# Dividing attention's outputs instead of its score blocks, pairing outputs, and loading the mask sizes on GpSimd's queue, in a fused attention and two-layer FFN kernel

## The chip, the cores and the metric

The kernel runs on one core of one Trainium2 chip. A core has five engines that each run their own stream of instructions: TensorE (PE, matrix products), VectorE (DVE), ScalarE (ACT), GpSimd (POOL) and SyncE (SP, which here only issues DMAs). The metric is the device time of one execution in microseconds (us); lower is better.

## The reference

Local and global attention with a distance bias, followed by two feed-forward layers:

```python
scores = scale * np.matmul(q, k.transpose(0, 1, 3, 2))     # q, k, v: 2 x 8 heads x 768 x 64
keep = is_global | is_local        # k < n_global (8), or 0 <= q - k < n_local (96)
scores = np.where(keep, scores + bias, -1e9)               # bias = -slope[head] * distance
a = np.exp(scores - np.max(scores, axis=-1, keepdims=True))
a = a / (np.sum(a, axis=-1, keepdims=True) + 1e-09)
x = np.matmul(a, v)                                        # as 1536 tokens x 512
h = x @ w_in;  x = (h * sigmoid(h)) @ w_out                # 512 -> 2048 -> 512
h = x @ w_in2; return np.maximum(0.01 * h, h) @ w_out2     # again 512 -> 2048 -> 512
```

`n_global` and `n_local` are inputs that the kernel reads at run time, as 64-bit integers; the weights come as 64-bit floats. A branch at the end of the program computes the attention in another way for sizes that the fast path does not cover; it does not run here.

## The kernel before

**Attention.** The work is cut into 24 units: a batch, a third of its queries (256) and a pair of heads; unit n counts pairs of heads fastest, then thirds, then batches. A unit passes through these steps, each a function of the code:

- `ld_qk`, `ld_v` (L893, L920): SyncE's queue (and for the first unit's k ScalarE's) loads q, k and v for two units at a time.
- `st_T` (L936 to L951): TensorE turns q and k by four transposes (products with the identity) into the PSUM tile `pt`; ScalarE copies q into `qT` with its scale, ScalarE or VectorE copies k into `kT` (helper L222 or L224), and VectorE spreads k's first columns, the global ones, to the other blocks (L948) where the unit is in the first third.
- `st_S` (L979): the scores, eight products into two PSUM tiles `s`. Each reads only 64 of the partitions, one head's. In the same task the outputs of the unit two back (`LAG`) are formed right behind them, see `st_AV`.
- `st_P`: VectorE scans each of four score blocks (L1012: adds the mask and keeps the minimum of its negative, the maximum, in `nm`) into `A`; ScalarE takes the exp and its sum (L1019, `su`); VectorE forms the reciprocal `rs` (L1025, L1026), 128 queries by 4 blocks, and multiplies each block of A by its column (L1035).
- `st_A` (L1052): TensorE transposes A into `pa`; ScalarE or VectorE copies it to `AT` (four buffers).
- `st_AV` (L1078): 6 or 8 products of v and `AT` into `pv`, 64 x 256 for each head, one head in the upper and one in the lower half of the partitions. ScalarE copies that to the high part of the layers' input `x` (L1090), VectorE the rest, `pv` minus the high part, to the low part (L1093).

**Layers.** Products are formed in three passes over high and low parts, in tiles `ph` (L600, first product of a layer), `po` (L655, second) and `pq` (L490, a form with fewer products). The weights are loaded by SyncE's queue into `st`, and brought to a high and a low part by ScalarE and VectorE (L273 to L288).

**Opening.** GpSimd builds the identity and the mask's constants; SyncE's queue loads q of the first unit, then n (`load_n`, L79, two DMAs into `nraw`), then more. VectorE makes floats of n in five small steps (`masks_n`, L828 to L832), then the mask (L839, L840, L843, L844). TensorE, with nothing to do yet, runs dummy products of zeros into `wps` (`warm_up`, L878): eight before the first transposes, two and one behind the first and the second unit's, and 16 more that the planner puts where TensorE would wait.

**Order.** A planner in Python (`Sched`) holds each task with its engine, an assumed duration, a priority (lower first; mostly the unit's number plus an offset), what it depends on and which buffers it needs. It plays the program through with these durations and writes each engine's order; that order is fixed when the program is built. A priority or an assumed duration thus changes only the order.

Of the kernel before, what the change touches and what calls it, by code (L numbers as in the profile page):

```python
# [26 lines left out]
def kernel(  # L27
# [40 lines left out]
    ident = const.tile([P, P], F32, name="ident")  # L68
    make_identity(nc, ident)

    warm = const.tile([P, 1], F32, name="warm")
    nc.vector.memset(warm, 0.0)
# [25 lines left out]
    def flags():  # L98
        nc.vector.tensor_scalar(fl[:, 0:1], nlf, 1.0, None, op0=ALU.is_lt)
        nc.vector.tensor_scalar(fl[:, 1:2], nlf, float(NPV + 1), None, op0=ALU.is_gt)  # L100
        nc.vector.tensor_scalar(fl[:, 2:3], ngf, float(NG), None, op0=ALU.is_gt)
        nc.vector.tensor_reduce(fl1, fl, axis=mybir.AxisListType.X, op=ALU.max)
        nc.vector.tensor_copy(flag, fl1)

    PASSES = ((0, 0), (1, 0), (0, 1))
    LAG = 2
    ADEPS = 0.1

# [11 lines left out]
    class Sched:  # L120
# [7 lines left out]
        def add(self, eng, dur, fn, prio, deps=(), bufs=(), at=0.0, land=ADEPS, dma=False):  # L128
            t = {"eng": (eng,) if isinstance(eng, str) else eng, "dur": dur if isinstance(dur, tuple) else (dur,),
                 "fn": fn, "prio": prio, "deps": [d for d in deps if d is not None], "bufs": bufs, "at": at,  # L130
                 "land": land, "dma": dma or eng == "SP", "out": [], "i": len(self.tasks), "state": 0}
# [8 lines left out]
        def run(self):  # L140
# [3 lines left out]
            for t in self.tasks:  # L144
                for e in t["eng"]:
                    free.setdefault(e, 0.0)
                    ready.setdefault(e, [])
# [4 lines left out]
            seq, dma = 0, 0.0  # L152
# [11 lines left out]
            now = 0.0  # L164
            while len(order) < len(self.tasks):
                for e in free:
# [20 lines left out]
                    end = free[e] = now + t["dur"][t["eng"].index(e)]  # L187
# [40 lines left out]
    class Moe:  # L228
# [233 lines left out]
        def unit_quad(self, ns, L, pair):  # L462
# [19 lines left out]
            def prod(c, A, Bx, first, deps=()):  # L482
# [15 lines left out]
                for kk in range(2):  # L498
                    m = add("PE", 3 * (0.2267 if two else 0.1185), fn(kk), self.pos, (wd, m, *Bx[kk][1], *deps), (wt_, bank[c], Bx[kk][0]))
# [83 lines left out]
        def unit_in(self, n, j, c0=0, w=TG):  # L583
# [42 lines left out]
            for kk in range(NKK):  # L626
                xd = [q for (a0, a1, q) in self.xdone[L][gi][kk] if a0 < c0 + w and c0 < a1]
                last = add("PE", 3 * 0.2267 * r, mm(kk), self.pos, (wt, last, *xd), (wb, ph, xs[kk]))
# [7 lines left out]
        def unit_out(self, n, e, c0=0, w=TG):  # L636
# [22 lines left out]
            for j in range(FPP):  # L659
                wb, wt = self.w["out", L, part * FPP + j]  # L660
                g, gt = self.g[n, j]
                m = add("PE", 3 * 0.2267 * r, mm(j), self.pos, (m, wt, *gt), (po, wb, g))
# [112 lines left out]
    SIZES = {"st": 2, "f": 4, "wi": 4, "wo": 4, "g": 4, "t": 2, "ps": 8, "qT": 3, "A": 2, "AT": 4, "tl": 4, "gl": 2,  # L775
# [9 lines left out]
    with ExitStack() as es:  # L785
# [10 lines left out]
        apool = lambda name, bufs=1: ea.enter_context(tc.tile_pool(name=name, bufs=bufs))  # L796
# [3 lines left out]
        sm = apool("sm", 4)  # L800
# [312 lines left out]
        for n in range(NU - LAG, NU):  # L1113
            st_AV(n)[2](None)
# [151 lines left out]
```

## Time and profile before

| | us |
|---|---|
| three runs | 607.74, 605.6, 605.74 |
| median of the runs | 605.74 |
| span of the profiled execution | 606.2 |
| TensorE busy in it | 596.1 (98%) |
| VectorE busy | 528.4 (87%) |
| ScalarE busy | 305.4 (50%) |
| GpSimd busy | 3.7 (1%) |

The profile is one execution, recorded by the hardware. A line number with an L is a line of the kernel before. A timeline row gives when an instruction or a row of equal ones starts and how long it takes; in square brackets stands the engine's idle time before it and who released it. An engine that appears as SPq or ACTq is its queue issuing DMAs. "PEld" is the loading of TensorE's stationary operand, which overlaps its products. The chain of waits is followed back from the last instruction, at each step to what released it.

### The profile page before, as it was taken

To read this page: it belongs to the slowest core of one execution; us is meant where nothing else is said; L and a number is where in the kernel's file an instruction comes from. 1 tells how busy PE (TensorE), PEld (TensorE's weight loads), DVE (VectorE), ACT (ScalarE), POOL (GpSimd) and SP (SyncE) were. 2 spreads that over 40 slices of the span, in tenths; PEclk is the share of its full clock that TensorE was granted. 3 is DMA by queue.
4 is the path that set the end of the run, shared out by engine and by line. 5 is a ranking of instruction groups with operands and counts; after the bars stand their busy time and mean duration, and the time that the engine had idled before them with its cause. 6 is when DMAs were issued, how large, how long until landed. Compare 5 with 4: busy or idle time off the path is not lost.

```text
span 606.2 us, 9115 instructions
## 1 busy us (share of the span) xinstructions
PE 596.1 (98%) x3266; PEld 490.0 (81%) x3267; DVE 528.4 (87%) x1213; ACT 305.4 (50%) x682; POOL 3.7 (1%) x20
## 2 busy tenths in 40 slices
PE   8999999999999999999999999999999999999996
PEld 4678777778888888888888888898898889888985
DVE  4999999877999999995999999899999997978551
ACT  4789887876654435432555554556343433333110
POOL 2000000000000000000000000000000000000000
PEclk9999999999999999999999999999999999999999
DMA  8875568310012332322231111322132322010112
GB/s 180 185 174 141 136 167 203 71 36 1 0 36 70 105 105 69 106 69 70 69 105 35 36 35 36 105 69 85 54 105 71 104 70 69 6 65 1 70 55 90
DMA packets 72676, 49.43 MB, mean 82 GB/s; under 512 B 50480, under 2 KB 67120, under 8 KB 72624
## 3 DMA queue, kind: packets, MB, share of 16 engines
q1 hardware_dynamic: 71536, 48.51, 28.6%
q8 instruction: 28, 0.46, 0.3%
q10 hardware_dynamic: 1088, 0.26, 0.2%
q14 instruction: 24, 0.20, 0.1%
HBM read 45.62 MB, written 3.15 MB: 80 GB/s over the span
## 4 chain that ended last, share of the span: by engine, by line
PE 94%; DVE 3%; DMA 2%; ACT 1%; issue 0%; ACTq 0%
PE po L655 43%; PE pq L490 29%; PE ph L600 10%; PE s L979 3%; PE pa L1052 3%; PE pv L1078 3%; PE pt L936 2%; DMA st<-in_moe_w_in_dram 1%; DVE A L1012 1%; PE wps L878 1%; DMA q<-in_q_dram 1%; DVE A L1035 0%; DMA k<-in_k_dram 0%; ACT AT L222 0%; ACT A L1019 0%; DVE f L279 0%
## 5 line engine op out<-in xcount | busy, mean ns | idle before, releaser
L655 PE MATMUL po<-g,wo 128*128 128x512 f32 x576 | 141.5, 392 | 0.0
L655 PE MATMUL po<-wo,g 128*128 128x512 f32 (+1 forms) x588 | 136.2, 385 | 0.0
L655 PEld LDWEIGHTS po<-wo,g 128*128 128x128 f32 x588 | 107.7, 188 | 21.0
L655 PEld LDWEIGHTS po<-g,wo 128*128 128x128 f32 x576 | 106.9, 188 | 21.7 <-DVE wo L288 0.2
L600 PE MATMUL ph<-x,wi 128*128 128x512 f32 (+1 forms) x336 | 77.6, 366 | 0.9 <-DVE wi L288 0.6
L505 DVE TENSOR_TENSOR tl<-tl,pq 128x512 f32<-128x512 f32 (+1 forms) x110 | 64.3, 585 | 10.3 <-PE pq L490 5.3
L600 PEld LDWEIGHTS ph<-x,wi 128*128 128x128 f32 x336 | 56.4, 188 | 11.0 <-DVE wi L288 1.2
L490 PE MATMUL pq<-xs,ws 128*128 128x512 f32 x252 | 62.3, 389 | 0.0
L490 PEld LDWEIGHTS pq<-xs,ws 128*128 128x128 f32 x252 | 47.3, 188 | 9.8
L273 ACT ACTIVATE st<-st 128x512 f32<-128x512 f32 x64 | 42.9, 670 | 23.5 <-DMA st<-in_moe_w_out_dram 13.2
L1019 ACT ACTIVATE A<-A,nm 128x256 f32<-128x256 f32 (+1 forms) x96 | 46.1, 483 | 12.1 <-DVE nm L1012 11.9
L687 DVE SCALAR_TENSOR_TENSOR yp<-po,yp 128x512 f32<-128x512 f32 x60 | 40.7, 686 | 9.4 <-PE po L655 9.1
L279 DVE SCALAR_TENSOR_TENSOR f<-st,f 128x512 int32<-128x512 int32 x64 | 43.9, 687 | 0.9
L282 DVE SCALAR_TENSOR_TENSOR f<-st,f 128x512 int32<-128x512 int32 x64 | 43.8, 684 | 0.4
L575 ACT ACTIVATE g<-tl 128x512 fp32r<-128x512 f32 x40 | 25.0, 630 | 37.5 <-DVE tl L570 29.0
L490 PE MATMUL pq<-xn,wi 128*128 128x512 f32 (+1 forms) x192 | 43.1, 336 | 0.0
L1012 DVE CUSTOM_DVE_ANT_0 A<-s,mask 128x256 f32<-128x256 f32 (+1 forms) x96 | 34.7, 393 | 3.9 <-PE s L979 3.7
L222 ACT ACTIVATE wo<-f 128x512 fp32r<-128x512 f32 x30 | 18.9, 630 | 34.6 <-PE po L655 17.2
L490 PEld LDWEIGHTS pq<-xn,wi 128*128 128x128 f32 x192 | 32.3, 189 | 4.5
L578 DVE TENSOR_TENSOR g<-tl,g 128x512 fp32r<-128x512 f32 x40 | 27.1, 686 | 5.1 <-ACT g L575 4.8
L575 ACT ACTIVATE g<-t 128x512 fp32r<-128x512 f32 x32 | 20.1, 630 | 19.7 <-PE po L655 10.8
L276 DVE TENSOR_SCALAR f<-st 128x512 int32<-128x512 int32 x64 | 26.7, 420 | 1.6 <-ACT st L273 1.6
(119 smaller groups left out, 883.2 us busy)
## 6 DMA issues: line engine op xcount, KB each, us to landing
st<-in_moe_w_in_dram SPq DMA_DIRECT2D x32, 512.0 KB, 3.8
st<-in_moe_w_out_dram SPq DMA_DIRECT2D x32, 512.0 KB, 3.6
vd<-in_v_dram SPq DMA_DIRECT2D x24, 128.0 KB, 2.8
q<-in_q_dram SPq DMA_DIRECT2D x22, 128.0 KB, 3.1
k<-in_k_dram SPq DMA_DIRECT2D x22, 128.0 KB, 3.4
out_dram<-yo SPq DMA_DIRECT2D x11, 256.0 KB, 2.1
vp<-in_v_dram SPq DMA_DIRECT2D x20, 96.0 KB, 2.7
vp<-in_v_dram SPq DMA_DIRECT2D x20, 32.0 KB, 2.4
```

Of the source, the lines that this page charges most:

```text
L273: eng.activation(hf, hf, AF.Copy, scale=2.0 ** -112)
L279: eng.scalar_tensor_tensor(fi(), lo(), 29, fi(), op0=ALU.logical_shift_right, op1=ALU.bitwise_or)
L282: eng.scalar_tensor_tensor(fi(), hi(), -(2 ** 31), fi(), op0=ALU.bitwise_and, op1=ALU.bitwise_or)
L490: eng.matmul(bank[c]()[:, :w], wt_()[:, a, f0:f0 + P], x()[:, b, c0:c0 + w], start=(first and kk == 0 and i == 0), stop=(kk == 1 and i == ...
L505: eng.tensor_tensor(dst[0]()[:, dst[1]], a[0]()[:, a[1]], b[0]()[:, b[1]], op=op)
L575: eng.activation(g()[:, 0, :], t(), AF.Copy)
L578: eng.tensor_tensor(g()[:, 1, :], t(), g()[:, 0, :].bitcast(F32), op=ALU.subtract)
L600: eng.matmul(ph()[:, :w], wv[:, a, kk, :], xs[kk]()[:, b, cs], start=(kk == 0 and i == 0), stop=(kk == NKK - 1 and i == 2),)
L655: eng.matmul(po()[:, :w], lhsT, rhs, start=(j == 0 and i == 0), stop=(j == FPP - 1 and i == 2))
L687: eng.scalar_tensor_tensor(dst()[:, cs], po()[:, :w], scale, y()[:, cs], op0=ALU.mult, op1=ALU.add)
L1012: eng.tensor_tensor_reduce(A()[:, i, j, c0:256], s[j]()[:, i, c0:256], mask0 if c0 else mask, -QSCALE * SLOPE[2 * hp + j], 3.0e38, ALU.add ...
L1019: eng.activation(a, a, AF.Exp, bias=nm()[:, x:x + 1], scale=-1.0, accum_out=su()[:, x:x + 1])
```

## The change

1. **n** is loaded by GpSimd's queue, in the first two instructions of its program, and no longer by SyncE's.
2. **Early first scores.** The dummies around the second unit's transposes are two of 256 columns ahead and one of 512 behind, instead of three of 512 behind; the first unit's k is copied by VectorE; dummies are products with a broadcast 128-column tile of zeros, and so the fill of zeros is shorter.
3. **Division.** A is no longer multiplied by the reciprocal. It is transposed as the exp left it. A new step `st_R` transposes `rs` on TensorE (`pr`, 4 x 128), copies it on ScalarE (`rT`), sends it to DRAM (`rd`) by a DMA on GpSimd's queue and reads it back by two more, each spreading two rows over 64 partitions (`R`, 128 x 256, three buffers). VectorE multiplies the output in `pv` by `R`, ScalarE copies the product to the high part of `x`, VectorE forms the low part from it.
4. **Paired outputs.** From unit 12 on the outputs of two units are formed in one task, behind every second unit's scores; the last pair stands alone. `AT` has six buffers instead of four.
5. **Planner.** Scans get the priority n - 1.63 (n + 0.1 before), other offsets, assumed durations and due times of weights change, and the planner counts a price for going from one kind of product to another.

```diff
+    nraw = const.tile([P, 2, 2], I32, name="nraw")
+    def load_n(eng, x):
+        eng.dma_start(out=nraw[:, x], in_=(n_global, n_local)[x].bitcast(I32).partition_broadcast(P))
+    for x in range(2):
+        load_n(nc.gpsimd, x)
     ident = const.tile([P, P], F32, name="ident")
     make_identity(nc, ident)
-    def load_n(eng):
-        for x, src in enumerate((n_global, n_local)):
-            eng.dma_start(out=nraw[:, x], in_=src.bitcast(I32).partition_broadcast(P))
...
+    SOLO = 24
+    PAIRS = 12
+    COLD = 6.5
+    SWITCH = {"fs": 0.095, "sv": 0.2, "vf": 0.17, "vs": 0.15, "fv": 0.1, "sf": 0.1}
...
-    SIZES = {"st": 2, "f": 4, "wi": 4, "wo": 4, "g": 4, "t": 2, "ps": 8, "qT": 3, "A": 2, "AT": 4, "tl": 4, "gl": 2,
+    SIZES = {"st": 2, "f": 4, "wi": 4, "wo": 4, "g": 4, "t": 2, "ps": 8, "qT": 3, "A": 2, "AT": 6, "R": 3, "tl": 4, "gl": 2,
...
-        nload = add("SP", 0.9, lambda eng: load_n(eng), -13.0, (), (), land=0.1)
-        zero = kp.tile([P, TG], mybir.dt.bfloat16, name="zero")
+        zero = kp.tile([P, P], mybir.dt.bfloat16, name="zero")
-        def warm_up(n):
+        def warm_up(n, w=TG):
             def fn(eng):
                 for _ in range(n):
-                    eng.matmul(wps(), zero[:, 0:P], zero, start=True, stop=True)
+                    eng.matmul(
+                        wps()[:, 0:w], zero, zero.rearrange("p (o c) -> p o c", o=1).to_broadcast([P, w // P, P]),
+                        start=True, stop=True,
+                    )
...
-            kd = add(AD, (0.42, 0.42), ev_k, n - 1.2, (t,), (pt, kt))
+            kd = add(AD if n else "DVE", (0.42, 0.42) if n else 0.42, ev_k, n + -2.08 if n else -1.5, (t,), (pt, kt))
...
-            av = st_AV(n - LAG) if n >= LAG else None
+            n = us[0]["n"]
+            if n < PAIRS:
+                av = st_AV(units[n - LAG:n + 1 - LAG]) if n >= LAG else None
+            else:
+                av = st_AV(units[max(n - LAG - 1, PAIRS - LAG):n + 1 - LAG]) if (n - PAIRS) % 2 else None
...
-                    r = add("DVE", 0.24 if c0 else 0.36, ttr, n + 0.1, (m, mtask), (s[j], A, nm))
-                    ex.append(add("ACT", 0.42 if c0 else 0.51, exp, n + 0.2, (r,), (A, nm, su)))
+                    r = add("DVE", 0.24 if c0 else 0.36, ttr, n + -1.63, (m, mtask), (s[j], A, nm))
+                    ex.append(add("ACT", 0.42 if c0 else 0.51, exp, n + 0.64, (r,), (A, nm, su)))
...
-                    def norm(eng, i=i, j=j, c0=c0):
-                        a = A()[:, i, j, c0:256]
-                        eng.tensor_scalar(a, a, rs()[:, 2 * i + j:2 * i + j + 1], None, op0=ALU.mult)
-                    u["norm"].append(add("DVE", 0.26, norm, n + 0.3, (rt,), (A, rs)))
+        def st_R(u):
+            ...
+            def mm(eng):
+                eng.transpose(pr(), rs(), ident)
+            def ev(eng):
+                copy(eng, rT(), pr())
+            def hop(eng):
+                eng.dma_start(out=rd(), in_=rT())
+            def spread(eng):
+                for j in range(2):
+                    eng.dma_start(out=R()[j * D:(j + 1) * D], in_=rd()[2 * j:2 * j + 2].rearrange("i t -> (i t)").partition_broadcast(D))
+            m = add("PE", 0.06, mm, n + 0.95, (u["rt"],), (rs, pr))
+            m = add("ACT", 0.26, ev, n + 1.1, (m,), (pr, rT))
+            m = add("POOL", 0.55, hop, n + 1.1, (m,), (rT, rd), land=0.1, dma=True)
+            u["Rd"] = add("POOL", 1.1, spread, n + 1.1, (m,), (rd, R), land=0.7, dma=True)
...
-                    def hi(eng, x=x, y=y):
-                        eng.activation(x()[:, 0, o:o + 256], pv()[:, y], AF.Copy)
-                    def lo(eng, x=x, y=y):
-                        eng.tensor_tensor(x()[:, 1, o:o + 256], pv()[:, y], x()[:, 0, o:o + 256].bitcast(F32), op=ALU.subtract)
+                    def norm(eng, R=R, y=y):
+                        eng.tensor_tensor(R(), pv()[:, y], R(), op=ALU.mult)
+                    def hi(eng, x=x, R=R, o=o):
+                        eng.activation(x()[:, 0, o:o + 256], R(), AF.Copy)
+                    def lo(eng, x=x, R=R, o=o):
+                        eng.tensor_tensor(x()[:, 1, o:o + 256], R(), x()[:, 0, o:o + 256].bitcast(F32), op=ALU.subtract)
+                    f = add("DVE", 0.36, norm, n + 2.01, (t, u["Rd"]), (pv, R))
+                    h = add("ACT", 0.35, hi, n + 3.11, (f,), (R, x))
+                    u["end"] = add("DVE", 0.36, lo, n + 0.71, (h,), (R, x))
...
-                add("PE", 0.5, warm_up(2 - u["n"]), -3.0, (u["T"],), (wps,))
+                add("PE", 0.22, warm_up(2 - u["n"], 256 if u["n"] == 0 else TG), 0.06 if u["n"] else -3.0, (u["T"],), (wps,))
...
-        for n in range(NU - LAG, NU):
-            st_AV(n)[2](None)
+        for n in range(NU - LAG - (NU - PAIRS) % 2, NU, 2):
+            st_AV(units[n:n + 2])[2](None)
...
-                return 3.5 + 1.2 * j if which == "in" else 8.0 + 1.3 * j
-            return 30.0 + 8 * (L * NPART + part) + (4 if which == "out" else 0) + j
+                return 4.46 + 1.2 * j if which == "in" else 9.0 + 1.3 * j
+            return 25.79 + 8 * (L * NPART + part) + (4 if which == "out" else 0) + j
```

How the instructions stand on an engine is shown at four places; a row names line, operation, output and inputs, and shape. First TensorE behind its first eight dummies, in the kernel before; two more dummies like the last one follow, then the first scores.

```order
L936 MATMUL pt<-ident,q 128x128 x2
L936 MATMUL pt<-ident,k 128x128 x2
L936 MATMUL pt<-ident,q 128x128 x2
L936 MATMUL pt<-ident,k 128x128 x2
L878 LDWEIGHTS zero
L878 MATMUL wps<-zero 128x512
```

The same place now:

```order
L953 MATMUL pt<-ident,q 128x128 x2
L953 MATMUL pt<-ident,k 128x128 x2
L892 LDWEIGHTS zero
L892 MATMUL wps<-zero 128x256
L892 LDWEIGHTS zero
L892 MATMUL wps<-zero 128x256
L953 MATMUL pt<-ident,q 128x128 x2
L953 MATMUL pt<-ident,k 128x128 x2
L892 LDWEIGHTS zero
L892 MATMUL wps<-zero 128x512
L996 MATMUL s_204<-kT,qT 128x128
```

Two dummies of half the columns have moved ahead of the second unit's transposes, one stands behind them, and the scores follow.

Second, VectorE in the opening, from the last of the five small steps on n to the first scan of a score block (an ISA row), in the kernel before:

```order
L832 TENSOR_SCALAR m8nl<-nf 128x1
L839 TENSOR_SCALAR mk<-mk,m8nl 128x256
L840 TENSOR_TENSOR mask<-mk 128x256
L948 COPY kT<-kT 128x5x32
L843 COPY mask<-mk 128x32
L844 TENSOR_TENSOR mask_119<-mask,mk 128x128
L948 COPY kT<-kT 128x5x32
L1012 ISA A,nm<-s_198,mask_119 128x128
```

and now:

```order
L842 TENSOR_SCALAR m8nl<-nf 128x1
L233 COPY kT<-pt 128x2x128
L849 TENSOR_SCALAR mk<-mk,m8nl 128x256
L850 TENSOR_TENSOR mask<-mk 128x256
L965 COPY kT<-kT 128x5x32
L853 COPY mask<-mk 128x32
L854 TENSOR_TENSOR mask_122<-mask,mk 128x128
L965 COPY kT<-kT 128x5x32
L1035 ISA A,nm<-s_204,mask_122 128x128
```

The copy of the first unit's k from `pt` has come to VectorE, between the steps on n and the mask.

Third, TensorE at the scores of unit 15 (`s`, the number is the tile's) and the outputs behind them. Before, the outputs are unit 13's:

```order
L979 MATMUL s_1429<-kT,qT 128x128
L979 MATMUL s_1431<-kT,qT 128x128
L979 MATMUL s_1429<-kT,qT 128x256
L979 MATMUL s_1431<-kT,qT 128x256
L1078 MATMUL pv<-AT,vd 64x128 x2
L1078 MATMUL pv<-AT,vp 64x128 x2
L1078 MATMUL pv<-AT,vd 64x128 x2
L936 MATMUL pt<-ident,q 128x128 x2
L936 MATMUL pt<-ident,k 128x128 x2
```

Now they are those of the units 12 and 13:

```order
L996 MATMUL s_1464<-kT,qT 128x128
L996 MATMUL s_1466<-kT,qT 128x128
L996 MATMUL s_1464<-kT,qT 128x256
L996 MATMUL s_1466<-kT,qT 128x256
L1117 MATMUL pv<-AT,vd 64x128 x2
L1117 MATMUL pv<-AT,vp 64x128 x2
L1117 MATMUL pv<-AT,vd 64x128 x4
L1117 MATMUL pv<-AT,vp 64x128 x2
L1117 MATMUL pv<-AT,vd 64x128 x2
L953 MATMUL pt<-ident,q 128x128 x2
```

and at unit 16's scores none follow:

```order
L1063 MATMUL pr<-ident,rs 4x128
L1093 MATMUL pa<-ident,A 128x128 x6
L664 MATMUL po<-g,wo 128x512 x3
L996 MATMUL s_1539<-kT,qT 128x256
L996 MATMUL s_1541<-kT,qT 128x256
L996 MATMUL s_1539<-kT,qT 128x256
L996 MATMUL s_1541<-kT,qT 128x256
L953 MATMUL pt<-ident,q 128x128 x2
L953 MATMUL pt<-ident,k 128x128 x2
```

Outputs of two units stand behind every second unit's scores; at the units between, the transposes of q and k follow the scores. `pr` stands beside the transposes of A.

Fourth, VectorE at the end of the attention. Before:

```order
L224 COPY AT<-pa 128x512
L1093 TENSOR_TENSOR x<-pv,x 128x256
L1025 TENSOR_SCALAR rs<-su 128x4
L1026 RECIPROCAL rs<-rs 128x4
L1035 TENSOR_SCALAR A<-A,rs 128x256 x4
L1093 TENSOR_TENSOR x<-pv,x 128x256
L224 COPY AT<-pa 128x512
L1093 TENSOR_TENSOR x<-pv,x 128x256
L376 TENSOR_TENSOR tl<-x 128x512 x3
```

and now:

```order
L1135 TENSOR_TENSOR R<-pv,R 128x256
L285 TENSOR_SCALAR f<-st 128x512
L288 SCALAR_TENSOR_TENSOR f<-st,f 128x512
L624 SCALAR_TENSOR_TENSOR t<-t,ph 128x512
L1141 TENSOR_TENSOR x<-R,x 128x256
L291 SCALAR_TENSOR_TENSOR f<-st,f 128x512
L632 TENSOR_TENSOR g<-t,g 128x512
L1135 TENSOR_TENSOR R<-pv,R 128x256
L1141 TENSOR_TENSOR x<-R,x 128x256
L1135 TENSOR_TENSOR R<-pv,R 128x256
L624 SCALAR_TENSOR_TENSOR t<-t,ph 128x512
L1141 TENSOR_TENSOR x<-R,x 128x256
```

Each multiplication of A has gone; an output is multiplied by `R` before its low part is formed, and steps on weights (`f`) and on the first layer (`t`, `g`) stand between these.

## Rows read from the trace of the kernel before

**Rows 1.** Page part 1, TensorE and the others: busy time, share of the span, instructions.

```profile
PE 596.1 (98%) x3266; PEld 490.0 (81%) x3267; DVE 528.4 (87%) x1213; ACT 305.4 (50%) x682; POOL 3.7 (1%) x20
```

**Rows 2.** Windows: stretch, length, busy us (instructions) by engine, PEclk, DMA share, GB/s.

```profile
60.00:80.00 20.00, 20.00 (x152) 15.41 (x152) 19.51 (x69) 16.43 (x50) 0.00 (x0) 1.00 0.59 153
...
600.00:607.00 7.00, 0.34 (x3) 0.13 (x2) 0.42 (x1) 0.00 (x0) 0.00 (x0) 0.80 0.24 82
```

**Rows 3.** Timeline of TensorE, 0 to 36: start, duration, line, tile, count, idle before.

```profile
1.21 3.60 PE L878 MATMUL wps<-zero 128*128 128x512 bf16 x8 [1.21 <-DVE zero L868]
...
4.60 0.64 PE L936 MATMUL pt<-ident,q 128*128 128x128 f32 x2
...
5.03 0.63 PE L936 MATMUL pt<-ident,k 128*128 128x128 f32 x2
...
6.35 0.79 PE L936 MATMUL pt<-ident,q 128*128 128x128 f32 x2 [0.69 <-DMA q<-in_q_dram]
...
8.77 2.31 PE L979 MATMUL s<-kT,qT 64*128 64x128 f32 x16
...
15.83 0.93 PE L979 MATMUL s<-kT,qT 64*128 64x128 f32 x8
...
33.71 1.13 PE L979 MATMUL s<-kT,qT 64*128 64x256 f32 x8
```

**Rows 4.** Timeline of the other engines and their queues, 0 to 17, same columns.

```profile
0.73 0.21 POOL masks.py:197 MEMSET ident<- 128x128 f32 x1 [0.29 <-POOLq L1249]
...
2.24 0.43 SPq L79 DMA_DIRECT2D nraw<-in_n_local_dram  x1
...
5.80 0.17 DVE L828 CAST npair<-nraw 128x4 f32<-128x4 int32 x1 [4.64 <-DMA nraw<-in_n_local_dram]
...
5.98 0.47 ACT L951 ACTIVATE qT<-pt,qsc 128x256 f32<-128x256 f32 x1
...
6.86 0.41 DVE L839 TENSOR_SCALAR mk<-mk,m8nl 128x256 f32<-128x256 f32 x1
...
7.64 0.25 DVE L948 COPY kT<-kT 128x160 f32<-128x160 f32 x1
...
10.46 0.29 DVE L1012 CUSTOM_DVE_ANT_0 A<-s,mask 128x128 f32<-128x128 f32 x1 [1.51 <-PE s L979]
...
12.07 0.49 ACT L1019 ACTIVATE A<-A,nm 128x256 f32<-128x256 f32 x1
```

**Rows 5.** Groups by line and shape: busy us, mean ns, then idle before and releasers.

```profile
L1035 DVE TENSOR_SCALAR A<-A,rs 128x256 f32<-128x256 f32 x80 | 23.3, 347 | 0.1
...
L1093 DVE TENSOR_TENSOR x<-pv,x 128x256 fp32r<-128x256 f32 x24 | 10.0, 417 | 2.2 <-ACT x L1090 2.2
...
L1019 ACT ACTIVATION_READ_ACCUMULATOR A<-A,nm 128x1 f32 x96 | 18.3, 191 | 0.0
```

**Rows 6.** Chain that ended last, by time: start us, us, what, count.

```profile
11.67 2.16 PE wps L878 x10
...
50.76 2.50 PE ph L600 x21
...
88.67 0.85 PE s L979 x8
...
89.52 0.81 PE pv L1078 x12
...
126.59 0.87 PE pa L1052 x8
...
128.86 1.06 PE s L979 x8
...
130.95 0.59 PE pt L936 x4
```

**Rows 7.** DMA issues: line, queue, count, KB each, median us to landing.

```profile
out_dram<-yo SPq DMA_DIRECT2D x11, 256.0 KB, 2.1
...
nraw<-in_n_local_dram SPq DMA_DIRECT2D x1, 1.0 KB, 3.5
```

More of the change, by code (lines that the diff above doesn't have):

```diff
@@ L163, in run @@
                         enter(t)
-            now = 0.0
+            now = 0.7
             while len(order) < len(self.tasks):
@@ L186, in run @@
                     order.append(t)
-                    end = free[e] = now + t["dur"][t["eng"].index(e)]
+                    end = now + t["dur"][t["eng"].index(e)] * (2.0 if e == "PE" and now < COLD else 1.0)
+                    if e == "PE" and t["mode"] != mode:
+                        end += SWITCH[mode + t["mode"]]
+                        mode = t["mode"]
+                    free[e] = end
                     heapq.heappush(ev, (end, -1, 2))
@@ L800 @@
         sm = apool("sm", 4)
+        dp = apool("turn", 4, space=bass.MemoryType.DRAM)
         late_pool = []
@@ L991, in st_S @@
                     bufs += av[1]
-                t = add("PE", 0.15 + 0.41 * (2 if us[0]["id"][1] else 1.5) * len(part), mm(part), part[0]["n"] + 0.0,
-                        deps, bufs, land=0.0)
-                us[0]["S"] = t
+                t = add("PE", sum(0.864 if u["id"][1] else 0.656 for u in part), mm(part), part[0]["n"] + 0.0,
+                        deps, bufs, land=0.0, mode="s")
+                for u in us:
+                    u["S"] = t
             if av:
                 av[2](t)
-            st_P(us[0])
+            for u in us:
+                st_P(u)
         def st_P(u):
@@ L1084, in go @@
                 n = us[0]["n"]
[L1085 removed]
+                t = add("PE", sum(0.872 if u["id"][1] else 0.654 for u in us), fn, -20.0 if after[0] else n + 1.5, (*deps, *after),
+                        bufs, mode="v")
                 for y, u in enumerate(us):
[L1087 to L1097 removed]
+                    b, sb, hp = u["id"]
+                    t0 = b * NSB + sb
+                    o = (t0 % 2) * 256
+                    x = xt[t0 // 2][hp]
+                    R = u["R"]
+                    def norm(eng, R=R, y=y):
[7 more added lines that the diff above has]
+                    u["end"] = add("DVE", 0.36, lo, n + 0.71, (h,), (R, x))
+                    xdone[t0 // 2][hp].append((o, o + 256, u["end"]))
             return deps, bufs, go
[L1101 removed]
+        add("PE", 1.6, warm_up(8), -9.0, (), (wps,), at=1.0)
         for x in range(16):
```

139 lines of the change are left out of this document (70 added, 69 removed).

## The prediction

> **What bounds the kernel now.** I read the shares of the page first, then the busy time by stretch, then TensorE in order of time. TensorE is busy 98% of the span [rows 1], and from 60 to 80 us, for one stretch behind the opening, in all of the 20 us [rows 2]: there VectorE, ScalarE and the DMAs only have to keep up, and an instruction saved on them is worth nothing. So I treat the span as TensorE's useful work plus the time that TensorE loses, and ask of each edit which of the two it changes. The losses lie in two places. One is the end: after 600 us TensorE has 0.34 us of work left [rows 2], and that tail (last output, store) is not touched. The other is the opening. The third unit's score block (scores are formed per unit, a pair of heads by 256 queries) starts only at 15.83 us, and 17.88 us later, at 33.71, the seventh [rows 3]; before the third, TensorE fills gaps with dummy products into `wps` that serve nothing. The profiled span is 606.2 us, 0.46 above the median of the runs, 605.74; I apply the sum to the median.
>
> **The opening, to the third scores.** Before, VectorE reaches the first scan of a score block at 10.46: it has waited 1.51 us for the scores, which stand on TensorE behind the second unit's transposes and three dummies and start at 8.77 [rows 3, 4]. After, two dummies of 256 columns stand ahead of the second unit's transposes and one of 512 behind them. Step by step: the first transposes stay at 4.60 and end at 5.66 [rows 3]; two half dummies, 0.45; the second unit's transposes, as long as the first's, 1.06; one dummy, 0.45: scores from 7.6 us. (The second unit's transposes waited for their q until 6.35 [rows 3]; its issue stood behind n's two on SyncE's queue and now comes 0.9 earlier, so it is there by 5.5.) The dummies' pace is that of the eight at 1.21, 0.45 each [rows 3]. The scores also need q and k. ScalarE copies q from 5.7, when the transposes end, to 6.17 (0.47); k's copy, now VectorE's, waits for ScalarE in the written order and is of q's shape, so it ends by 6.64; two mask steps and the broadcast of k's first columns follow, together 1.03 (from 6.86 to 7.64 + 0.25 before) [rows 4], so to 7.7. The scores' second half waits for that. By TensorE's count the first scan follows the start at 7.6 as before, 1.69 us later, at 9.3. The floor is 8.3: the broadcast at 7.7, half a score block at the pace it has later (0.85 for a block [rows 6]), 0.15 to the scan. I take 8.8, the middle, because it is open when TensorE changes level there: ten dummies at 11.67 take 2.16 us, eight at 1.21 take 3.60 [rows 3, 6], the higher against the lower of its two levels (2.4 and 1.2 GHz), and the window's clock column does not show the change.
>
> All this needs the masks' input n early enough. VectorE's copy of n waits until 5.80 now, the five small steps from there take 1.06, to 6.86 [rows 4], and k's copy now stands behind them. GpSimd's queue issues n as its first work, where the identity stood at 0.73; with issues like SyncE's (0.43) and landings of 2.1 to 3.5 us by the nearest rows [rows 4, 7], n lands at 3.7 to 5.1. Up to 5.1 it hides behind q's copy (5.1 + 1.06 = 6.17), later each us costs a us. GpSimd's identity and constants move back by the two issues, 0.9; the first transposes start 3.9 us behind the identity's old start, which covers that.
>
> From the first scan to the third scores it was 5.37 us (10.46 to 15.83 [rows 3, 4]). Now the exps no longer lead through the reciprocal and four multiplications by it before the transposes. From the first scan to the end of the fourth exp it took 2.1 (10.46 to 12.56 [rows 4]); with a copy of k among them, 0.4, 2.5. Then transposes of the second block, 4 x 0.109 (0.87 for eight [rows 6]); three dummies, 0.65; the new transpose `pr` of the reciprocals, 0.11; two dummies, 0.43. That is 4.1. Third scores at 12.9 instead of 15.83: **-2.9 us**. Ends: -3.4 (first scan at 8.3), and -1.3 (scan at 9.3, and the five dummies in this path still at the lower level, 0.23 more each).
>
> **Third to seventh scores.** By TensorE's own steps [rows 6] the old 17.88 us hold four transposes of q and k (2.36), two score blocks of 0.85 and two of 1.06 (3.82), four outputs of 0.81 (3.24), 26 transposes of A (2.83) and 18 passes of `ph` (2.14): 14.4, so 3.5 us were lost to VectorE and ScalarE. After, the order puts only three `ph` passes there, four more transposes of A, four `pr` and five dummies: useful 13.5. VectorE sheds per unit four multiplications of A (0.347 each, 23.3 in all for the 80 wide ones) and gains one of the output, priced as its neighbour of the same shape (0.417, 10.0 in all) [rows 5]: at least 13 us less. ScalarE gains `rT`, 4x128, between 0.19 and 0.49, an accumulator read and a 256-column exp [rows 4, 5], 5 to 12 us in all. Following the queues, a unit is now TensorE's 3.2 to 3.4 us (scores, outputs, transposes) plus what scores wait for their q, 0.2 to 0.6: four units with the dummies 15.6. Lost 2.1 instead of 3.5: **-1.4 us**; the `ph` passes that are missing come later, so they are no gain. Ends: -2.4 (only the dummies are lost) and 0 (the old loss stays).
>
> **Behind that, TensorE's work itself counts.** It gains 24 transposes `pr` of a 128x4 block; the first is in the path above. The other 23 at 0.109, the step of A's transposes: **+2.5**. Half of that is the other end, since four columns are loaded where those load 128; I take the measured row. It sheds changes between score, output and plain products. Their price: four transposes of q and k behind outputs take 0.59 instead of 4 x 0.109, so 0.15 for output to plain; score blocks take 1.06 with 1024 columns and 0.85 with 768, so 0.21 per 256 and 0.21 left over for score to output [rows 6]. The third kind I take between. From unit 12 on six pairs save one change each and the last pair two: 8 x 0.18, **-1.4** (-1.2 to -1.7). The rest of the planner's changes (durations, two more `AT` buffers, due times) only reorder work that TensorE does in any case; from 60 to 80 VectorE is busy 19.51 us and ScalarE 16.43 [rows 2]; VectorE's cover grows, ScalarE's shrinks by about 1 us in 20 where it has 3.6 idle. I cost that at nothing; with the cover gone each late q would cost TensorE its wait.
>
> Sum: -2.9 - 1.4 + 2.5 - 1.4 = -3.2, so **602.5 us**. The terms' ends together reach -6.2 and 0.
>
> **Rivals.** *`pr` is a change of its own (slower).* TensorE's records name a tile for each product: 128*128, 64*128 for scores, 128*64 for outputs, and each change between them costs 0.15 to 0.21. If a stationary of four columns were one more such tile, nearly every `pr` would pay two changes: 46 x 0.18 = 8.3, of which about 1 falls into lost time: 609.5. It decides from 0.15 us above my price per `pr` on. Against it: in the built program the load of `rs` names the whole column group, like that of A, where the outputs' loads name a half. Chance 0.12. The Trainium skill, TensorEngine Tiling (Array Packing), Key Properties, says that a change of tiling mode drains the engine; by that rule alone `pr` would pay, and the trace agrees for scores and outputs. The same page, Restrictions, says that column tiling and FP32 transposes exclude each other, which takes `pr` out of the rule; no row here shows it.
>
> *The reciprocal comes back late.* `rs` now goes TensorE, ScalarE, DRAM, and back spread over the partitions by three GpSimd DMAs, the last two behind the first's landing: 2.1 to 3.5 us each way by the nearest landings [rows 7]; with issues and two units queued I estimate 8 to 9.5. VectorE multiplies the output by it in its place in the queue, with exps' scans and A's copies behind. For most units that place is two units (some 9 us) later; for the last two only some 6 us of VectorE work lie between. There VectorE waits 2 to 3.5, the products that read the last outputs stand nine passes (2.0 us) behind them, and TensorE loses about as much: 605.5 (604.5 to 607). Chance 0.14. The Trainium skill, SBUF — State Buffer, The "DVE blocks DMA" trap, says that GpSimd cannot write its DMAs' descriptors while VectorE runs a double-rate single-source step; whether these DMAs would wait no row here shows, since GpSimd issues none before.
>
> *n is late and the scores are not early.* If GpSimd's two issues or landings take 2 us more, k's copy, the scores and the scan all move by 2: 604.5 (603.5 to 605.7). Chance 0.12.
>
> **How the numbers follow.** Forecast 0.62, most of it 599.8 to 604.5. About 0.5%, 3.0 us, is what a measurement of this kernel can tell from no change: faster is below 602.7, slower above 608.8. Of the forecast I put two thirds below 602.7, since VectorE's relief can also take back losses behind the seventh scores that the sum leaves alone, and the rest within; the two late cases lie within; `pr` as a change lies above. Faster 0.42, within 0.46, slower 0.12. The range 599.8 to 606.5 leaves out the first rival and the forecast's lower tail.
>
> **What would show it.** Right: first scan near 8.8 and third scores near 13 us; a `pr` next to plain products adding about 0.1 us; six stretches with 24 or 32 output passes in a row; no wait of VectorE on the spread reciprocal; TensorE full in 60:600. Wrong: `pr` rows with 0.4 us between their neighbours; VectorE waiting for a DMA at the multiplication of the output, above all near the end of the attention; a copy of n that starts after 6 us; dummies at 0.43 us each up to the third scores.

## The result

The changed kernel takes 611.88 us (median of 4 runs, 611.39 to 614.67) against 606.0 for the kernel before: 1.0102 times, 95% interval 1.0079 to 1.0124. It is slower by about 6 us, where 602.5 was forecast. Where a run lists both, its time is 1.7 to 2.1 us longer than its span, so spans compare with spans and times with times; the profiled execution of the changed kernel has a span of 609.6 us.

The profile after, page part 1 (busy time and its share by engine):

```profile
PE 597.0 (98%) x3291; PEld 492.9 (81%) x3291; DVE 515.6 (85%) x1149; ACT 307.6 (50%) x698; POOL 43.1 (7%) x94
```

VectorE is 12.8 us less busy than in [rows 1] and TensorE has about the same busy time, but TensorE's last product ends at 603.5 and not at 600.3. So time was lost on TensorE, and not in the opening. The timeline of the changed kernel there, TensorE's scores first, then VectorE (start us, duration us, what, idle before):

```profile
7.98 1.76 PE L996 MATMUL s<-kT,qT 64*128 64x256 f32 x12 [0.33 <-DVE kT L965]
13.39 0.93 PE L996 MATMUL s<-kT,qT 64*128 64x128 f32 x8
...
28.72 1.50 PE L996 MATMUL s<-kT,qT 64*128 64x256 f32 x8
```

```profile
5.75 0.17 DVE L838 CAST npair<-nraw 128x4 f32<-128x4 int32 x1 [4.82 <-DMA nraw<-in_n_local_dram]
...
8.96 0.29 DVE L1035 CUSTOM_DVE_ANT_0 A<-s,mask 128x128 f32<-128x128 f32 x1
```

The first scan is at 8.96 (10.46 in [rows 4]), the third unit's scores at 13.39 and the seventh's at 28.72 (15.83 and 33.71 in [rows 3]). The opening came out nearly as forecast (8.8, 12.9 and 28.5). Where it went from there is in the windows (stretch, length, busy us of PE, PEld, DVE, ACT, POOL, granted clock, DMA share, GB/s):

```profile
28.72:48.00 19.28, 19.28 (x181) 16.14 (x181) 17.76 (x66) 18.07 (x58) 6.23 (x12) 1.00 0.92 209
48.00:66.00 18.00, 15.24 (x124) 12.75 (x124) 14.05 (x49) 12.89 (x39) 4.18 (x8) 0.91 0.64 156
66.00:140.00 74.00, 71.99 (x585) 56.30 (x584) 59.66 (x211) 61.18 (x195) 22.23 (x42) 1.00 0.56 138
```

TensorE is full from 28.72 to 48 us; then it stands idle for 2.76 us within 18, and for 2.01 in the 74 behind. In the table of waits (engine and line, what it waited for: us in total, times, longest) the new one is VectorE's on the spread reciprocal:

```profile
DVE R L1135 <- DMA R<-rd: 9.1, 8, 2.0
```

The first two of these eight waits, in the timeline of GpSimd's queue, ScalarE and VectorE:

```profile
38.51 0.27 ACT L231 ACTIVATE rT<-pr 4x128 f32<-4x128 f32 x1
39.06 0.52 POOL L1069 DMA_DIRECT2D rd<-rT  x1 [3.70 <-DMA rd<-rT]
...
42.47 0.27 ACT L231 ACTIVATE rT<-pr 4x128 f32<-4x128 f32 x1 [0.18 <-PE pr L1063]
42.50 1.03 POOL L1073 DMA_DIRECT2D R<-rd  x2 [1.49 <-DVE rs L1049]
...
43.51 0.52 POOL L1069 DMA_DIRECT2D rd<-rT  x1
...
48.38 0.42 DVE L1135 TENSOR_TENSOR R<-pv,R 128x256 f32<-128x256 f32 x1 [1.59 <-DMA R<-rd]
...
50.65 1.05 POOL L1073 DMA_DIRECT2D R<-rd  x2 [6.62 <-DVE f L288]
...
55.85 0.42 DVE L1135 TENSOR_TENSOR R<-pv,R 128x256 f32<-128x256 f32 x1 [1.99 <-DMA R<-rd]
```

One unit's reciprocal is copied at 38.51, leaves at 39.06, is spread from 42.50 on, and VectorE gets it at 48.38: 9.9 us. The next is copied at 42.47; its way out can leave only behind the spread of the one before (GpSimd's queue is in order), at 43.51; its spread starts at 50.65, 7.1 us later, and VectorE gets it at 55.85: 13.4 us. The profile names VectorE's step on weights as what ended GpSimd's 6.62 us idle; but the buffer of this spread, that of three spreads before, had been free since about 39.8, when VectorE had formed the low part from it, so I read the wait as that for the way out. Over all units the landings are (first the way out, then the spread; min, median, max):

```profile
DMA to landing us min/median/max: 1.6/3.8/6.6
```

```profile
DMA to landing us min/median/max: 2.5/3.1/5.3
```

The chain that ended last, in this stretch (start us, duration us, what):

```profile
43.00 5.29 DMA R<-rd
...
51.19 4.57 DMA R<-rd
...
55.85 0.44 DVE R L1135
...
56.33 1.33 PE ph L609 x9
57.66 1.84 PE s L996 x8
59.50 1.88 PE pv L1117 x16
```

The DMA leads to VectorE's multiplication, and that to TensorE's `ph`. The last two rows show a second price: scores of 1024 columns take 1.84 us instead of 1.06 [rows 6], the outputs 1.88 instead of the 1.02 that 16 of them take elsewhere in the chain, 1.64 us more together. The window shows the clock there (same columns):

```profile
58.00:60.00 2.00, 2.00 (x14) 1.25 (x12) 1.94 (x8) 2.00 (x7) 0.65 (x2) 0.50 0.51 107
```

The granted clock is 0.50, the lower of the two levels (1.2 of 2.4 GHz), after TensorE had stood idle 0.85 us before 52.46 and 1.63 us before 56.33.

### The profile page after: what moved, and what is told of

It is laid out like the page before. It is cut to its first block, busy times and chain, and to the rows that moved or that the text cites. A ratio compares the mean times of both kernels' runs of the same rounds, so it can differ in the third digit from the quotient of the medians.

```text
span 609.6 us, 9321 instructions
## 1 busy us (share of the span) xinstructions
PE 597.0 (98%) x3291; PEld 492.9 (81%) x3291; DVE 515.6 (85%) x1149; ACT 307.6 (50%) x698; POOL 43.1 (7%) x94
## 3 DMA queue, kind: packets, MB, share of 16 engines
q1 hardware_dynamic: 71248, 48.51, 28.5%
## 4 chain that ended last, share of the span: by engine, by line
PE 86%; DMA 6%; DVE 5%; issue 1%; POOL 1%; ACT 1%; DVEq 0%; POOLq 0%; ACTq 0%
PE po L664 41%; PE pq L499 29%; PE ph L609 9%; DMA R<-rd 4%; PE s L996 2%; PE pv L1117 2%; PE pa L1093 1%; DMA rd<-rT 1%; DVE A L1035 1%; PE pt L953 1%; DMA nraw<-in_n_local_dram 1%; POOL R L1073 1%; PE wps L892 1%; DVE R L1135 0%; ACT A L1042 0%
## 5 line engine op out<-in xcount | busy, mean ns | idle before, releaser
L1035 DVE CUSTOM_DVE_ANT_0 A<-s,mask 128x256 f32<-128x256 f32 (+1 forms) x96 | 33.4, 396 | 8.6 <-PE s L996 8.6
L1073 POOL DMA_DIRECT2D R<-rd x48 | 25.5, 536 | 52.2 <-DVE nm L1035 13.4
```

Source lines behind the costliest of these rows:

```text
L1035: eng.tensor_tensor_reduce(A()[:, i, j, c0:256], s[j]()[:, i, c0:256], mask0 if c0 else mask, -QSCALE * SLOPE[2 * hp + j], 3.0e38, ALU.add ...
L1073: eng.dma_start(out=R()[j * D:(j + 1) * D], in_=rd()[2 * j:2 * j + 2].rearrange("i t -> (i t)").partition_broadcast(D))
```

## The experiments

The theory (W): VectorE multiplies by the reciprocal in a fixed place of its queue, the reciprocal comes back later than that, and everything queued behind is late; the forecast's other terms are right. Rivals: the new products `pr` and the new order cost TensorE by themselves (P); the added DMAs disturb the weights' loads (D).

### Nothing waits for the reciprocal

```diff
-                    eng.dma_start(out=R()[j * D:(j + 1) * D], in_=rd()...
+                    eng.dma_start(out=dump[j * D:(j + 1) * D], in_=rd()...
...
-                        eng.tensor_tensor(R(), pv()[:, y], R(), op=ALU.mult)
+                        eng.tensor_tensor(R(), pv()[:, y], one, op=ALU.mult)
```

> The changed kernel, with every instruction kept in its order, but VectorE multiplies the output by a tile of ones, and the two DMAs that spread the reciprocal write to a tile that nobody reads. So the division is left out of the result; nothing waits for the reciprocal's return. Theory W (VectorE waits in its queue for R, and all that is queued behind it is late): the 9.1 us of VectorE's waits on R are gone, TensorE is full from 40 to 140 us to within 1 us, and the time falls to 602 to 604.5 us. Theory P (the new transposes and the reordered products cost TensorE by themselves): the time stays at 609 or above, and TensorE's losses between 40 and 140 us stay near 4.3 us. Theory D (the extra DMAs and GpSimd's descriptors disturb the weights' loads): stays at 609 or above as well, with waits on weights in place of those on R.

Measured: 604.14 us (before 606.32 on this chip; ratio 0.9964, 0.995 to 0.9978), 7.7 less than the changed kernel. The same three stretches of the trace:

```profile
28.84:48.00 19.16, 19.16 (x181) 16.09 (x181) 18.77 (x69) 18.02 (x58) 6.54 (x13) 1.00 0.92 202
48.00:66.00 18.00, 17.32 (x153) 15.00 (x152) 16.91 (x59) 16.17 (x51) 5.04 (x10) 1.00 0.74 196
66.00:140.00 74.00, 73.96 (x586) 58.48 (x585) 62.58 (x211) 62.09 (x191) 21.86 (x41) 1.00 0.52 131
```

TensorE's idle time from 48 to 140 us falls from 4.77 to 0.72 us and the clock stays at 1.00. Of the 6.6 us between the two spans (609.6 and 603.0), 4.05 are idle time and 1.64 the lower clock; the rest, some 0.9, is not attributed. `pr`, the order and every DMA are still there (the spreads now go to one tile), and ScalarE's waits for weights are no shorter, 25.3 us against 23.1; so P and D fall, and W stands.

### The multiplication later in the queue

```diff
-                        end = max(end, dma) + 1.7
+                        end = max(end, dma) + (4.2 if e == "POOL" else 1.7)
...
-    ... "AT": 6, "R": 3, ...
+    ... "AT": 6, "R": 6, ...
```

> The changed kernel, but the planner reckons 2.5 us more for each DMA on GpSimd's queue (about 10 us from the start of the reciprocal's way to its return in place of 5), and R has six buffers. It then places the multiplication of the output later in VectorE's queue. Theory W: waits on R fall below 3 us and the time to 603 to 606 us; if the outputs, now formed into x later, hold up the first products of the first layer instead, 606 to 609. Theories P and D: 609 or above.

Measured: 607.16 us, ratio 1.001 (0.9999 to 1.0021). The wait on R is gone from VectorE's table, and 4.7 of the 7.7 us with it; the best of the range was missed. TensorE now loses elsewhere, 1.14 us of it here (0.21 in the changed kernel):

```profile
20.00:40.00 20.00, 18.86 (x168) 14.45 (x165) 19.56 (x69) 17.31 (x58) 8.03 (x16) 1.00 1.06 205
```

VectorE is busy 19.56 of 20 us there, but in the changed kernel 19.48, with as many steps on weights (9). TensorE's waits from 20 to 48 us are for ScalarE and VectorE, 0.5 us and less in each row of the table; which step of the new order costs it is not shown. So a planner that reckons a longer way back removes the wait, but not at no price.

### The division on A again

```diff
+                    u["norm"].append(add("DVE", 0.26, norm, n + -0.15, (rt,), (A, rs)))
...
-                m = add("PE", 0.22 if c0 else 0.44, mm, n + 1.46, u["ex"][2 * i:2 * i + 2], (A, pa))
-                if i:
-                    st_R(u)
+                m = add("PE", 0.22 if c0 else 0.44, mm, n + 1.46, u["norm"][2 * i:2 * i + 2], (A, pa))
```

> The changed kernel, but the division is on A again as in the kernel before (four multiplications on VectorE per unit, no pr, rT, rd, R); the early first scores, the paired outputs, six AT buffers and the planner's numbers stay. Theory W and the prediction's own sums of the other parts: third scores near 14 us, pairs save 1.4 us, no pr: 602 to 604.5 us. If the gain in the opening came from the division's way only (A not waiting for the reciprocal): 604.5 to 606.5. If pairing or the reordering itself is what costs: 608 or above.

Measured: 608.0 us, ratio 1.0029 (1.0016 to 1.0042), outside what I expected of the theory and just at what the last case named. In the trace TensorE waits longest for VectorE's multiplications of A (VectorE's first scan, TensorE's scores of the third and the seventh unit, then TensorE's largest wait in the whole run):

```profile
9.11 0.29 DVE L1035 CUSTOM_DVE_ANT_0 A<-s,mask 128x128 f32<-128x128 f32 x1
...
14.52 0.93 PE L996 MATMUL s<-kT,qT 64*128 64x128 f32 x8
...
33.38 1.13 PE L996 MATMUL s<-kT,qT 64*128 64x256 f32 x8
```

```profile
PE pa L1101 <- DVE A L1059: 3.0, 5, 0.9
```

From first scan to third scores it takes 5.41 us, against 4.43 in the changed kernel; from third to seventh scores 18.9, against 15.3 in the changed kernel and 17.9 before. That fits a gain made of what the division's move frees on VectorE. But dividing A also comes later here than before, behind the scans with their high priority; that is my reading of the order, and it was not tried apart.

### SyncE's queue for the reciprocal

```diff
-            m = add("POOL", 0.55, hop, n + 1.1, (m,), (rT, rd), land=0.1, dma=True)
-            u["Rd"] = add("POOL", 1.1, spread, n + 1.1, (m,), (rd, R), land=0.7, dma=True)
+            m = add("SP", 0.5, hop, n + 1.1, (m,), (rT, rd), land=0.1, dma=True)
+            u["Rd"] = add("SP", 1.0, spread, n + 1.1, (m,), (rd, R), land=0.7, dma=True)
```

> The changed kernel, but the reciprocal's DMAs, out and back, are issued by SyncE's queue. If the long way comes from GpSimd's queue (out 3.3 to 7.1 us, back 2.5 to 5.3 us in the trace of the changed kernel), both fall to the 2.1 to 2.6 us that stores of the output take, and the time to 603 to 606 us. If it comes from the load of the DMA engines by the weights, the ways stay as long, SyncE's loads wait behind them, and the time is 610 to 614 us.

Measured: 609.77 us, ratio 1.0056 (1.0039 to 1.0073): between the two cases. VectorE still waits on R:

```profile
DVE R L1135 <- DMA R<-rd: 6.6, 10, 1.1
```

6.6 us instead of 9.1, and now loads of weights and q stand behind the reciprocal's DMAs on SyncE's queue. The landings of this queue are not in the trace, so whether GpSimd's queue or the load lengthens the way is not settled by this run.

### The price of `pr`

```diff
-                eng.transpose(pr(), rs(), ident)
+                pr()
...
-                copy(eng, rT(), pr())
+                copy(eng, rT(), one[0:4, 0:P])
```

> The kernel e1_no_wait without the 24 products pr; ScalarE's copy takes a row of ones instead, so this leaves out the reciprocal's transposes as well as the division. All else keeps its order. TensorE is full there from 40 us on, so the difference to e1_no_wait (604.1 us) is the price of pr. By the prediction's term (0.109 us each): 2.6 us less, 601.5. By half that (four columns loaded): 1.3 less, 602.8. If each pr were a change of its own kind (0.18 us more on either side): about 8 to 10 us less, 594 to 596.

Measured: 601.2 us, 2.9 less than e1_no_wait (0.9917 of before, 0.9904 to 0.9931): 0.12 us for each of 24, next to the 0.109 of the forecast and far from what a change of tile would cost. The profile names the tile of `pr` 128*4, and yet the next product starts only 0.11 us behind it, at 12.87 (changed kernel):

```profile
12.76 0.27 PE L1063 MATMUL pr<-ident,rs 128*4 128x128 f32 x1
```

### The price of pairing

```diff
-    PAIRS = 12
+    PAIRS = 24
```

> The kernel e1_no_wait (no wait for the reciprocal, division left out) with the outputs of each unit formed on their own to the end, 24 groups in place of 17. By the prediction's term eight changes of 0.18 us come back: 1.4 us more than e1_no_wait, 605.5 (605.3 to 605.8). If pairing saves nothing, or costs by later outputs: 604.1 or less.

Measured: 605.07 us, 0.9 more than e1_no_wait (ratio to before 0.9976, 0.9967 to 0.9985). Pairing saves, as forecast. But the edit brings back six changes and not eight: the last loop still takes units by two, so there are 23 groups and the last pair stands in one row of 32 products:

```profile
126.06 0.44 PE L1120 MATMUL pv<-AT,vp 128*64 128x128 f32 x4
...
127.64 0.39 PE L1120 MATMUL pv<-AT,vd 128*64 128x128 f32 x4
```

That is 0.155 us for each of six, next to the 0.18 of the forecast, and at this price some 1.2 us for all eight.

### n by SyncE's queue

```diff
-    for x in range(2):
-        load_n(nc.gpsimd, x)
...
+        nload = add("SP", 0.9, lambda eng: [load_n(eng, x) for x in range(2)], -13.0, (), (), land=0.1)
```

> The kernel e1_no_wait with n loaded by SyncE's queue as in the kernel before; the dummies, k's copy and all priorities stay. In the trace of the changed kernel VectorE's copy of n starts at 5.75 us, against 5.80 before: if n by GpSimd brings nothing, the first scan stays at 9 us to within 0.2 and the time at 604.1 to within 0.6. By the prediction (n earlier by about 1 us, and needed): first scan and time about 1 us later, 605.1.

Measured: 604.59 us (0.9971 of before, 0.9961 to 0.998), 0.45 more than e1_no_wait, with intervals that overlap. VectorE's copy of n starts at 5.94, against 5.88 there, yet the first scan comes at 9.71, against 9.09. So n is no earlier by GpSimd's queue. The scan waited for the scores here:

```profile
8.03 2.68 PE L998 MATMUL s<-kT,qT 64*128 64x128 f32 x16
```

```profile
9.71 0.29 DVE L1037 CUSTOM_DVE_ANT_0 A<-s,mask 128x128 f32<-128x128 f32 x1 [0.54 <-PE s L998]
```

In e1_no_wait these 16 products take 0.49 and 1.75 us. The traced execution reached TensorE's higher level only at about 10 us (about 6.7 there), and at 605.77 us it is the slowest of its ten runs; q came 0.1 us later (TensorE waits for it until 6.47, against 6.35). So the scan's 0.6 us are not shown to be the queue's.

### The kernel before, a second trace

> The kernel before once more, for a second trace of it beside these, since the profiled execution of the first was 2 us longer than the median of its runs. Third scores at 15.8 us to within 0.3; TensorE's idle time up to 140 us 3.5 to 4.5 us; time 605.6 to 608.

Measured: 606.33 us, span 604.4. TensorE's transposes of k and its scores of the first, the third and the seventh unit:

```profile
4.98 0.38 PE L936 MATMUL pt<-ident,k 128*128 128x128 f32 x2
...
7.75 1.99 PE L979 MATMUL s<-kT,qT 64*128 64x128 f32 x16
...
14.36 0.93 PE L979 MATMUL s<-kT,qT 64*128 64x128 f32 x8
...
32.25 1.13 PE L979 MATMUL s<-kT,qT 64*128 64x256 f32 x8
```

This was not expected. In [rows 3] the same transposes of k take 0.63 us and the scores start at 8.77; here 0.38 and 7.75. TensorE reached its higher level at about 5 us here, and only at about 10 in the execution on which the prediction rests, during its 16 scores (2.31 us there, 1.99 here). With that the first scan (8.95 for 10.46) and the third and seventh scores come 1.5 us earlier in the same program, most of the 1.8 us between the two spans (604.4 and 606.2). In the changed kernel k's second transposes (at 6.63) take 0.38, so the level is up by then.

### Two versions after these runs

In the first the reciprocal goes to DRAM straight from VectorE's tile, without `pr` and `rT`:

```diff
-                eng.dma_start(out=rd(), in_=rT())
+                eng.dma_start(out=rd().rearrange("i t -> t i"), in_=rs())
```

> A version after the runs so far. The reciprocal goes from VectorE's tile straight to DRAM, 512 numbers written one by one in the other order, so pr (2.9 us by e5_no_pr against e1_no_wait) and rT fall away; the planner reckons 7 us for the way out and 3.2 for the way back more than the issue, forms the reciprocal earlier, and has R four and AT eight buffers, pairs from unit 10 on. If the scattered write lands within 7 us and VectorE does not wait for R: e2_later_R (607.2) less 2.9 and less its idle time up to 140 us (4.5 us against 2.8 in e1_no_wait): 602 to 604.5 us. If it takes longer (GpSimd writes 512 descriptors for it), VectorE waits for R as in the changed kernel: 608 or above.

Measured: 683.07 us (1.1254 of before). The second case, and far beyond it. The way out, 512 numbers of four bytes each, lands after (min, median, max)

```profile
DMA to landing us min/median/max: 8.0/10.7/16.8
```

and the spreads behind it land after 9.5 us in the median (3.1 in the changed kernel). ScalarE waits 53.9 us for weights (9.5 in the changed kernel), and VectorE 31.4 us for R:

```profile
ACT st L282 <- DMA st<-in_moe_w_in_dram: 53.9, 12, 23.3
...
DVE R L1133 <- DMA R<-rd: 31.4, 8, 9.0
```

The Trainium skill, DMA: Bandwidth & Descriptors, Specifications, gives 512 B as the least size at full rate, below which the DMA engine reads and writes back; four bytes are far below it, and the trace agrees that such writes are dear, not by which mechanism. Whether they themselves hold up the loads of weights, or the loads stand behind others in SyncE's queue, is not shown.

The second keeps the changed kernel's way for the first 12 units and divides A for the others:

```diff
+            if n >= HOPS:
+                        u["ready"].append(add("DVE", 0.34 if not c0 else 0.27, norm, n + -0.5, (rt,), (A, rs)))
...
-                if i:
+                if i and n < HOPS:
                     st_R(u)
```

> The changed kernel with the reciprocal's way for the first 12 units alone, where VectorE is the bound, and A divided on VectorE from unit 12 on, where it has 2 to 5 us of 20 idle; the planner reckons 2 us more for each of GpSimd's DMAs, R has four buffers, pr follows the reciprocal at once. Twelve pr less are worth 1.4 us (2.9 us for 24) against e2_later_R (607.2), and late waits on R cannot occur behind unit 12: 604.5 to 606 us. If the divisions of the late units hold up TensorE, as those of the early ones did in e3_divide_A: 607 or above.

Measured: 604.8 us (12 runs), ratio 0.998 (0.9968 to 0.9991): as expected, and the one version with a complete result that is faster than both kernels, by 1.1 us against the kernel before. From 80 us on, where A is divided, TensorE is full:

```profile
80.00:100.00 20.00, 20.00 (x155) 15.31 (x153) 17.91 (x65) 16.96 (x52) 0.00 (x0) 1.00 0.70 175
```

## Why the prediction was wrong

**The step that failed is "For most units that place is two units (some 9 us) later", set against the "8 to 9.5 us" estimated for the reciprocal's way.** By these two the sum had no wait on R in it, and the rival had one for the last two units alone, at a chance of 0.14 and 3 us. The rival's mechanism was right. But VectorE waits in eight of the 24 units, six times for 0.9 to 2.0 us and twice for less than 0.4, and the last two units are not among them. Both sizes were off: counted from ScalarE's copy into `rT`, VectorE stood at its multiplication after 6.3 to 8.3 us in five of these six units and after 11.4 in the sixth; the reciprocal was there after 7.2 to 10.0 us, and in the sixth after 13.4. The nearest of these places (same columns as in the timelines above):

```profile
124.80 0.25 ACT L231 ACTIVATE rT<-pr 4x128 f32<-4x128 f32 x1
125.33 0.53 POOL L1069 DMA_DIRECT2D rd<-rT  x1 [0.62 <-ACT rT L231]
...
131.99 0.42 DVE L1135 TENSOR_TENSOR R<-pv,R 128x256 f32<-128x256 f32 x1 [0.92 <-DMA R<-rd]
```

I had taken the way from lone transfers of 2.1 and 3.5 us [rows 7]; here each leg takes up to 6.6 or 5.3 us, and a unit's way out can stand on GpSimd's queue behind the spread of the unit before, which waits for its own way out (the unit behind the two shown in the result is copied at 47.91 and leaves at 51.69). The price, 7.7 us by e1_no_wait, has a part that the rival did not have: after the idle time TensorE ran for a while at half its clock (1.64 us). Rival and forecast together left 611.9 outside the range.

**The opening** came out within 0.5 us of its forecast: first scan 8.96 for 8.8, third scores 13.39 for 12.9, seventh 15.3 us later for 15.6. For the first scan that is luck. The forecast left out the steps that held it: GpSimd's two on the global columns' mask, which wait for n, and VectorE's behind them. First the changed kernel, then e0_before:

```profile
7.53 0.87 POOL L846 TENSOR_SCALAR mk<-mk,m8nl 128x128 f32<-128x128 f32 x1
...
8.44 0.18 DVE L853 COPY mask<-mk 128x32 f32<-128x32 f32 x1 [0.51 <-POOL mk L846]
```

```profile
8.43 0.18 DVE L843 COPY mask<-mk 128x32 f32<-128x32 f32 x1 [0.51 <-POOL mk L836]
...
8.95 0.29 DVE L1012 CUSTOM_DVE_ANT_0 A<-s,mask 128x128 f32<-128x128 f32 x1
```

So against an execution of the old kernel in which TensorE's level rises early, neither n's new queue nor the early scores moved the first scan. The execution that I measured against was late itself: against e0_before third scores gain 1.0 us and not 2.9. That 1.0 lies behind the first scan, 4.43 us instead of 5.41, and with the division on A (e3_divide_A) it is 5.41 again. I had noted that TensorE's level was open there and charged it to the range of the new kernel, not to the old one's, and then applied a sum made on a late execution to the median of all. I had also held its span, 606.2, against a median of times; like with like, it stood some 2 us above the median and not 0.46.

**n** was forecast at 3.7 to 5.1 us and is read at 5.75: GpSimd's second issue goes out at 1.93, not at about 1.2, and takes 3.7 us to land. The forecast had each us beyond 5.1 cost a us, and the first scan does hang on it: n's last small step ends at 6.71, GpSimd's two steps on the mask follow without a gap to speak of, to 8.40, and k's copy starts at 6.62, behind n's steps, and not at 6.17, behind q's. What was early is the start of the scores, 7.16 for 7.75 in e0_before, with two dummies fewer between it and the second unit's transposes. The second unit's q was not there by 5.5, though its issue came earlier: in e1_no_wait TensorE waits for it until 6.35.

**`pr`** was right (2.5 forecast for 23, 2.9 measured for 24), and so the rival of a further kind of tile fell (its 609.5 should by its own terms have been 609.8). The Trainium skill, TensorEngine Tiling (Array Packing), Restrictions, says that column tiling excludes FP32 transposes; e5_no_pr agrees with it, at 0.12 us a piece. **Pairing** was right and forecast a little large: 1.4, against some 1.2 at the price that e6_no_pairs gives.

With the wait taken away the sum, -3.2, stands against a measured -2.2 us (-3.0 to -1.3, e1_no_wait). That is close by luck: the opening is worth 1.9 less, `pr` 0.4 more dear, pairing 0.2 less, third to seventh 0.3 more, which makes about -1.0; the remaining 1.2 us no run attributes.

Still open: what makes the legs long. The longest way out (43.51 to 50.65) falls into a stretch in which the DMA engines are busy 0.81 of the time, and where they are busy 0.11 a way out takes 3.6 us to its spread (windows from the issue of a way out to its spread, same columns as in the result):

```profile
43.50:50.60 7.10, 6.82 (x70) 5.67 (x71) 5.48 (x21) 5.97 (x21) 0.53 (x2) 1.00 0.81 211
...
125.30:128.90 3.60, 3.60 (x47) 3.00 (x47) 2.15 (x11) 3.10 (x13) 0.53 (x2) 1.00 0.11 30
```

Five more such windows, at shares of 0.48 to 0.67, last 3.9 to 5.0 us. That fits a load by the weights, and no run took the load away. The Trainium skill, SBUF — State Buffer, The "DVE blocks DMA" trap, would have GpSimd's descriptors wait while VectorE runs a step in a two-port mode: GpSimd's issues last 0.52 to 0.64 us throughout, so they show no such wait, and a wait behind the issue this profile would not show.

## What to carry to other kernels

A step that leaves an engine and comes back by DMA has to be placed by its way in the kernel itself, both legs and the queue in which they stand one behind the other, and not by lone transfers: 5 us in the planner and 8 to 9.5 in my estimate were 7 to 13 where VectorE waited. And the place of the step that uses it has to be read from the order on its engine, unit by unit: 9 us as a rule were 6.3 to 8.3 in most of the units that waited. An in-order engine that waits for it holds up all that stands behind, and TensorE here paid twice, in idle time and then at a lower clock. And before a sum is made on one profiled execution, its time should be held against the other runs: this one was late in the very stretch that the change was to shorten.

## What the runs showed of the hardware that was not expected

- One program reaches TensorE's higher level at different times: about 5 us in one execution of the kernel before, about 10 in another, worth 1.5 us at the third scores; about 10 also in e7_n_sync, and about 6.6 in the changed kernel.
- TensorE fell to its lower level behind idle stretches of 0.85 and 1.63 us with some 2 us of work between them (changed kernel, granted clock 0.50 from 58 to 60 us).
- A 2 KB transfer by GpSimd's queue lands after 1.6 to 6.6 us, median 3.8. The Trainium skill, DMA: Bandwidth & Descriptors, Anatomy of one DMA — SWDGE (gpsimd) path, gives a fixed cost of about 2.0 us for this path; beside the weights' loads the trace has about twice that in the median; that the loads are the cause is not shown.
- A scattered write of 512 four-byte numbers lands after 8.0 to 16.8 us; the version with 24 of them took 683.07 us against 605.93.
